# Block maxima, head sums, early weights and step order in a fused attention and two-MoE kernel

## Chip, cores and metric

The kernel runs on one core of a Trainium2 chip, as one program. The metric is device time in microseconds (us), the median of several runs. The profile is one further execution, recorded by the hardware profiler. Engines are called PE (matmuls), DVE (vector), ACT (scalar activation), POOL (GpSimd) and SP (which issues the DMAs).

## What is computed

Three stages follow each other. Block-causal attention over 8 batches, 8 heads, 576 positions and head size 64, whose mask lets a position see its own 64-key block and those before it; its output, read as 4608 tokens of 512 numbers, goes through a soft mixture of experts with 32 slots; and that goes through a two-layer network whose activation is a scaled square of a relu.

```
scores = scale * q @ k.T;  scores = where(block_i >= block_j, scores, -1e9)
attn = softmax(scores);  x = attn @ v                     # 8 batches, 8 heads, 576 x 64
logits = x @ phi                                          # 4608 x 32
d = softmax(logits, over tokens);  slot_input = d.T @ x   # 32 x 512
for e in range(8):                                        # four slots each
    slot_out[e] = relu(slot_input[e] @ w1[e]) @ w2[e]
c = softmax(logits, over slots);  x = c @ slot_out
h = x @ w_in;  out = (s * relu(h) ** 2 + b) @ w_out
```

## The kernel before

**Attention in pairs.** The work of attention is cut into 32 pairs of heads, four pairs to each batch. For a pair, `rough` computes scores of 128-query chunks against the keys in reduced precision, in four pieces r0 to r3, `rough_max` (L289 to L303) takes their maxima on DVE, `rough_join` (L305) joins these into `mx`, and `m_row` turns them into rows `mT` that two small DMAs bring to `mr`. `score` (s0 to s3, L343) then computes the scores that count, `expo` (L350) the exponentials `pc` on ACT, `pv` (L397) the products with the values. POOL adds the exponentials up over keys in `S` (L365 and three pieces at L371 for each pair). The sums are split into two halves of lower precision, `sh` by ACT and `sl` by DVE (L258), and `dens` (L428) reduces them over partitions with matmuls. `tokens` (L415) turns outputs to rows of tokens and multiplies by phi, so that each head brings 64 output numbers and 32 partial logits. `norm` (L439 to L447) divides: `rs`, `rr`, then `xb` (128 rows, four token groups) and `xt` (the last 64 tokens of a batch).

**Maxima.** The maxima of whole 128-key blocks are taken over 128 rows into `mm`. Those 64-key blocks that only the upper 64 queries of a chunk may see are reduced over 64 rows, into the other half of the same tile. Piece r3 lies in the same tile as s1 (`PIG = 1`), and both its maximum on DVE and the exponential of s1 on ACT read that tile.

**Route.** When a batch is done, `route_s0` sums the partial logits of eight heads into `lgs` (L464, one reduce over `xb`, and in odd batches one over `xt`). `route_p` turns it and takes the maxima `mb` and `mt` and the running maximum `nrun`; `route_l` takes exponentials `ex`; `route_e` turns these into `d`; `route_x` multiplies `d` with `xb` and `xt` (L539, L542) and adds into `acc` (L544), with the running sum `ssum`. Odd batches have 128 tokens of two batches in `xt`, and so more of each.

**The order.** The steps of all pairs are written out by hand: `at(tau, ...)` puts each at a time tau, which is 8 for each pair plus an entry of the table `SLOT`, and `run` issues them in order of tau. Each engine works through its instructions in the order in which they were issued, and SP through its DMAs. The words of `w_in` are converted meanwhile, in 16 of the pairs (`wide_in`, ops `ag` and `wi`, L646 and L647 on ACT and L636 and L638 on DVE).

**Expert phase.** After attention, w1 and w2 of the experts (64 half tiles of 512 KB) are loaded by L113 into places that become free: four whole places `wlate`, allocated when attention's buffers are closed, and others after the last steps of attention. The first products with them are `hp` (L922).

Of the kernel before, what the change touches and what calls it, by code (L numbers as in the profile page):

```python
# [34 lines left out]
}  # L35

ON = {"k": "A", "q": "A", "sl": "D"}
# [6 lines left out]
def fused_kernel(  # L44
# [34 lines left out]
    wpre = wholes(ctx, "wpre", NPRE)  # L79

# [12 lines left out]
    wt = {}  # L93

# [48 lines left out]
    XB = rtp.tile([128, 4, 8, 96], F32, name="xb", bufs=1)  # L143
    XT = rtp.tile([128, 8, 96], F32, name="xt", bufs=1)
# [9 lines left out]
    KT, QT, RV = [None] * 3, [None] * 3, [None] * 3  # L154
    for i in (2, 0, 1):
        KT[i] = earlyp.tile([128, 640], F32, name=f"kt_{i}")
        QT[i] = earlyp.tile([128, 640], F32, name=f"qt_{i}")
        RV[i] = earlyp.tile([128, 5, 128], F32, name=f"rv_{i}")
# [3 lines left out]
    NB_ = {"pc": 5, "mT": 4, "ssp": 1}  # L162
# [12 lines left out]
    MM = [latep.tile([128, 2, 5, 2], F32, name=f"mm_{i}") for i in range(2)]  # L175
# [176 lines left out]
    def key_sum(p, c):  # L352
# [4 lines left out]
        if p == NP - 1 and c == 3:  # L357
            sh, sl = st["s3"] = [ring("s" + x, [128, 2, 576], F16)[:, :, 0:256] for x in "hl"]
# [75 lines left out]
    def norm(p):  # L434
# [5 lines left out]
        if p == NP - 1:  # L440
# [3 lines left out]
        DVE.tensor_tensor(out=XB[:, :, 2 * j:2 * j + 2, :], in0=ps[:, :, 0:384].rearrange("p h (u c) -> p u h c", u=4),  # L444
                          in1=rr[:, 0:4].to_broadcast([128, 4, 2, 96]), op=ALU.mult)

        DVE.tensor_tensor(out=XT[l0:l0 + 64, 2 * j:2 * j + 2, :], in0=ps[64:128, :, 384:480],  # L447
                          in1=rr[64:128, 4].to_broadcast([64, 2, 96]), op=ALU.mult)
# [86 lines left out]
    def route_x(b):  # L535
# [5 lines left out]
        if b % 2:  # L541
            PE.matmul(ps[0:32, :], d[:, 128:160], XT[:, :, 0:64], start=False, stop=True)  # L542
# [34 lines left out]
    for p in range(NP):  # L577
# [30 lines left out]
        A("norm", norm)  # L608
        A("mr", m_row)
    for b in range(NB):  # L610
        z = 8 * (4 * b + 3) + O["route"]
        if b == NB - 1:
            at(8 * (NP - 1) + O["den"] + 0.001, 8, route_s0, b, 0, 6)
            at(z + O["rh"], 8, route_s0, b, 6, 8)
        else:
            at(z + O["rh"], 8, route_s0, b)
# [8 lines left out]
    cvp = att.enter_context(tc.tile_pool(name="cvp", bufs=1))  # L625
# [634 lines left out]
```

## Time and profile before

| what | value |
|---|---|
| median of 3 runs | 843.72 us (843.55 to 844.74) |
| the profiled execution | 841.7 us, of which 839.9 are its span |
| PE busy | 780.2 us, 93% of the span |
| DVE, ACT, POOL busy | 681.7, 585.3, 220.2 us |
| attention, expert phase, rest | 0 to 356, 355.5 to 441.5, 442 to 840 us |

The busy shares are means over three stages with different limits, so they say little of one change. The rows below are read by stage: a window gives each engine's busy time in a stretch, a timeline the start and length of each group of instructions and, in brackets, how long its engine was idle before and on whom it waited.

### The profile page before, as it was taken

Reading aid. Unit: us, or ns where it says so; the run is one execution under the profiler, and the core shown is the slowest. Engines: PE = TensorE matmul, PEld = TensorE weight load, DVE = VectorE, ACT = ScalarE, POOL = GpSimd, SP = SyncE. Lnnn points to the kernel's source line nnn. Section 1 sums busy time; section 2 is a strip of 40 time slices with the busy share of each in tenths; the row PEclk is TensorE's granted clock in tenths of the full one; section 3 lists DMA queues with packets and bytes.
Section 4 is the critical chain, followed back from the end, with each engine's and each line's share of the span. In section 5 each row is a group of like instructions: output and inputs, shape, how many; then the busy total and the mean of one; then the engine's idle time right before and its main releaser. Section 6 shows DMA issues by size and latency. Waiting matters only on the chain.

```text
span 839.9 us, 18427 instructions
## 1 busy us (share of the span) xinstructions
PE 780.2 (93%) x7604; PEld 580.5 (69%) x7604; DVE 681.7 (81%) x1175; ACT 585.3 (70%) x848; POOL 220.2 (26%) x191
## 2 busy tenths in 40 slices
PE   4999989898989899967888889999999999999996
PEld 3666757575667575732314678888888888888885
DVE  5788888888888888669876788888888888888885
ACT  4766767575767666547876787777777877877771
POOL 3553534443535344402000011111111111111110
PEclk9999999999999999988899999999999999999999
DMA  4565543242434433299990000000000000000001
GB/s 144 196 211 181 196 145 96 81 159 101 157 133 146 146 96 96 82 385 407 397 392 9 1 26 27 26 27 26 27 26 27 26 27 26 27 26 27 26 27 51
DMA packets 40483, 92.97 MB, mean 111 GB/s; under 512 B 4624, under 2 KB 4944, under 8 KB 40400
## 3 DMA queue, kind: packets, MB, share of 16 engines
q1 hardware_dynamic: 40400, 91.80, 31.3%
q8 instruction: 60, 0.98, 0.5%
q14 instruction: 23, 0.19, 0.1%
HBM read 81.86 MB, written 9.44 MB: 109 GB/s over the span
## 4 chain that ended last, share of the span: by engine, by line
PE 77%; DVE 10%; DMA 8%; ACT 3%; issue 1%; POOL 1%; SPq 0%; POOLq 0%; DVEq 0%; ACTq 0%
PE s L343 13%; PE o L1121 13%; PE o L1123 12%; PE o L1122 12%; PE pv L397 9%; PE tp L415 4%; DMA w<-in_moe_w_dram 4%; PE s L286 4%; PE h L1084 4%; DMA w2h<-in_moe_w_dram 3%; DVE mm L272 3%; DVE lgs L464 2%; PE tp L428 2%; ACT rhl L1102 1%; PE hp L922 1%
## 5 line engine op out<-in xcount | busy, mean ns | idle before, releaser
L272 DVE TENSOR_REDUCE mm<-s 64x4 f32<-64x256 f32 (+5 forms) x224 | 139.1, 634 | 50.2 <-ACT pc L350 30.1
L1103 DVE TENSOR_TENSOR rhl<-G,rhl 128x1792 f16<-128x1792 f32 (+1 forms) x76 | 146.2, 1923 | 3.1 <-ACT rhl L1102 2.7
L350 ACT ACTIVATE pc<-s 128x896 f32<-128x896 f32 (+1 forms) x128 | 104.0, 838 | 58.7 <-PE s L343 30.4
L1085 ACT ACTIVATE r<-h 128x512 f32<-128x512 f32 x144 | 85.8, 596 | 60.8 <-PE h L1084 60.8
L343 PE MATMUL s<-qt,kt 64*128 64x448 f32 (+4 forms) x768 | 124.5, 416 | 1.2 <-DVE mm L272 0.5
L1102 ACT CAST rhl<-G 128x1792 f16<-128x1792 f32 (+1 forms) x76 | 121.0, 1592 | 5.4 <-DVE G L1095 5.3
L365 POOL TENSOR_TENSOR S<-pc 128x896 f32<-128x896 f32 x31 | 64.9, 2093 | 181.8 <-ACT pc L350 181.8
L1123 PEld LDWEIGHTS <-rhl 128*128 128x128 f16 x1008 | 98.8, 98 | 13.2 <-DVE rhl L1103 1.6
L1121 PEld LDWEIGHTS <-rhl 128*128 128x128 f16 x1008 | 98.8, 98 | 13.2
L1122 PEld LDWEIGHTS <-rhl 128*128 128x128 f16 x1008 | 98.8, 98 | 11.8
L397 PE MATMUL pv<-pc,rv 128*64 128x448 f32 (+4 forms) x768 | 100.3, 397 | 0.0
L371 POOL TENSOR_TENSOR S<-S,pc 128x640 f32<-128x640 f32 (+2 forms) x93 | 93.3, 1003 | 7.3
L343 PE MATMUL s<-mr,neg 64*128 64x448 f32 (+4 forms) x384 | 94.9, 487 | 0.0
L1140 POOL TENSOR_TENSOR z<-u,bdif 128x256 f32<-128x256 f32 x18 | 41.8, 2320 | 188.8 <-DVE u L1126 188.8
L1093 DVE TENSOR_TENSOR G<-G 128x512 f32<-128x512 f32 (+1 forms) x76 | 50.5, 665 | 46.5 <-ACT G L1092 46.0
L1092 ACT ACTIVATE G<-r 128x1024 f32<-128x1024 f32 (+1 forms) x76 | 76.9, 1011 | 2.2
L397 PEld LDWEIGHTS pv<-pc,rv 128*64 128x64 f32 x768 | 47.3, 136 | 32.1 <-issue 20.7
L343 PEld LDWEIGHTS s<-qt,kt 64*128 64x128 f32 x768 | 60.4, 188 | 7.4 <-DVE mm L272 2.9
L286 PE MATMUL s<-kr,qr 64*128 64x64 f32 (+4 forms) x384 | 54.0, 348 | 10.2 <-ACT kr L243 7.9
L286 PEld LDWEIGHTS s<-kr,qr 64*128 64x128 f32 x384 | 32.7, 191 | 40.2 <-ACT pc L350 21.1
L1084 PE MATMUL h<-ct,mst 128*128 128x256 f16 x288 | 55.2, 274 | 3.5 <-DVE mst L1049 1.3
L415 PEld LDWEIGHTS tp<-IP,ot 64*128 64x128 f32 x640 | 40.8, 188 | 17.3 <-ACT kr L243 7.3
(302 smaller groups left out, 1787.9 us busy)
## 6 DMA issues: line engine op xcount, KB each, us to landing
w<-in_moe_w_dram SPq DMA_DIRECT2D x36, 512.0 KB
w2h<-in_moe_w_dram SPq DMA_DIRECT2D x28, 512.0 KB
qt<-in_q_dram SPq DMA_DIRECT2D x32, 320.0 KB
kt<-in_k_dram SPq DMA_DIRECT2D x32, 320.0 KB
rv<-in_v_dram SPq DMA_DIRECT2D x32, 320.0 KB
wi<-in_moe_w_in_dram SPq DMA_DIRECT2D x8, 1024.0 KB
wo<-in_moe_w_out_dram SPq DMA_DIRECT2D x8, 1024.0 KB
out_dram<-ob SPq DMA_DIRECT2D x16, 256.0 KB
```

What stands on the lines that cost most here:

```text
L272: DVE.tensor_reduce(out=o, in_=i, axis=AX, op=ALU.max)
L286: PE.matmul(ps[:, h, o:o + k1 - k0], qt[a, 128 * j:128 * j + 128], kt[a, k0:k1], start=(n == 0), stop=(n == len(RG[r]) - 1))
L343: PE.matmul(ps[:, h, o:o + c1 - c0], a[r], b[r], start=(n == 0), stop=(n == 1))
L350: ACT.activation(out=pc[:, :, 0:w], in_=st.pop(("ps", p, c))[:, :, 0:w], func=AF.Exp, scale=scale)
L371: eng.tensor_tensor(out=x, in0=x, in1=pc[:, :, o:o + c1 - c0], op=ALU.add)
L397: PE.matmul(st["pv", p][r, x[0], x[1]], rv[:, sl, r], pc[:, h, o:o + c1 - c0], start=head, stop=(sl == 4 or c1 <= 128))
L1084: PE.matmul(hps[:, 256 * o:256 * o + 256], mst[:, 128 * f:128 * f + 128], ct[g], start=True, stop=True)
L1102: ACT.copy(rh, G)
L1103: DVE.tensor_tensor(out=rl, in0=G, in1=rh, op=ALU.subtract)
L1121: PE.matmul(o, rh[:, a, n], bh, start=first, stop=False)
L1122: PE.matmul(o, rh[:, a, n], bl, start=False, stop=False)
L1123: PE.matmul(o, rl[:, a, n], bh, start=False, stop=last)
```

## The change

Five things are changed.

1. The maxima of 64-key blocks are taken over 128 rows like the others, into a second half `me` of `mm`. `rough_join` becomes one op, the larger of `mm` and `me + mlow`, where `mlow` is -3e38 on the lower 64 rows; it has two inputs in SBUF.
2. `xt` becomes the fifth part of `xb`. A new step `head_sum` adds each pair's partial logits to `la` (pairs 1 to 3 of a batch, 24 adds on DVE, two inputs in SBUF), and `route_s0` is one add of the two halves of `la`. The pieces that the last batch had for this go.
3. Two of the four `wlate` places are allocated from the start, and two whole tiles of w1 (four half tiles) are loaded into them at pairs 26 and 27. Room is made with two buffers in place of three for `rv`, one in place of two for `ag` and for `ot`, and two in place of four for `mT`.
4. All entries of `SLOT` are new.
5. `slotT` is cleared by POOL instead of DVE, and the last pair's `sh` and `sl` of s3 stand in a buffer of `S`.

The diff, cut to its core; of the table a few entries stand:

```diff
 SLOT = {
...
-    5.18176, "sh1": 8.65626, "sl0": 6.52132, "sl1": 8.89128, "pv0": 3.67699, "pv1": 5.43325, "pv2": 5.43402, "pv3":
-    5.78017, "oc": 6.88883, "den": 10.19669, "norm": 11.64578, "route": 12.44301, "re": 2.40618, "rp": 0.37853,
...
+    9.33946, "sl0": 9.95287, "sl1": 10.51401, "pv0": 5.35704, "pv1": 7.37396, "pv2": 8.06025, "pv3": 8.15647, "oc":
+    9.07061, "den": 11.34750, "norm": 14.22647, "hs": 14.23143, "route": 10.06565, "re": 6.23354, "rp": 5.65308,
...
 }
+NEARLY = 2
-ON = {"k": "A", "q": "A", "sl": "D"}
+ON = {"k": "A", "q": "A", "sl": "D", "hs": "D", "xt": "D"}
...
+    wearly = wholes(ctx, "wearly", NEARLY)
...
-    XB = rtp.tile([128, 4, 8, 96], F32, name="xb", bufs=1)
-    XT = rtp.tile([128, 8, 96], F32, name="xt", bufs=1)
+    XB = rtp.tile([128, 5, 8, 96], F32, name="xb", bufs=1)
+    LA = rtp.tile([128, 5, 2, 32], F32, name="la", bufs=1)
...
-        mm, me = MM[p % 2][:, :, :, 0], MM[p % 2][64:128, :, :, 1]
-        by64 = ps[64:128].rearrange("p h (u c) -> p h u c", c=64)
+        mm, me = MM[p % 2][:, 0], MM[p % 2][:, 1]
+        by64 = ps.rearrange("p h (u c) -> p h u c", c=64)
...
-            rmax(me[:, :, 0:1], ps[64:128, :, 448:512])
+            rmax(me[:, :, 0:1], ps[:, :, 448:512])
...
-        rmax(MX[p % 2][:, 0:10], MM[p % 2].rearrange("p h j a -> p (h j) a"))
+        mm, me = (MM[p % 2][:, n].rearrange("p h j -> p (h j)") for n in range(2))
+        DVE.scalar_tensor_tensor(out=MX[p % 2][:, 0:10], in0=me, scalar=mlow[:, 0:1], in1=mm, op0=ALU.add, op1=ALU.max)
...
-        head_sum(lgs[:, gt(b):gt(b) + 4, :], XB[:, :, :, 64:96].rearrange("p u h n -> p u n h"))
-        if b % 2:
-            head_sum(lgs[:, gt(b) + 4, :], XT[:, :, 64:96].rearrange("p h n -> p n h"))
+    def head_sum(p):
+        b, j = p // 4, p % 4
+        if j == 0:
+            return
+        n = 4 + b % 2
+        x = XB[:, 0:n, 2 * j:2 * j + 2, 64:96]
+        eng = {"P": POOL, "D": DVE}["D" if p == NP - 1 else ON["hs"]]
+        eng.tensor_tensor(out=LA[:, 0:n], in0=XB[:, 0:n, 0:2, 64:96] if j == 1 else LA[:, 0:n], in1=x, op=ALU.add)
+    def route_s0(b):
+        n = 4 + b % 2
+        DVE.tensor_tensor(out=lgs[:, gt(b):gt(b) + n, :], in0=LA[:, 0:n, 0], in1=LA[:, 0:n, 1], op=ALU.add)
...
+    early = [split(t) for t in wearly]
+    for i, t in enumerate(early):
+        home["w1", i] = t
+        at(8 * (26 + i), 10, load_w, ("w1", i), t)
...
-    wlate = wholes(ctx, "wlate", 4, reuse_waits="tile")
+    wlate = wearly + wholes(ctx, "wlate", 4 - NEARLY, reuse_waits="tile")
...
-    at(8 * (NP - 1) + O["norm"] + 0.02, 9, DVE.memset, slotT, 0.0)
+    at(8 * (NP - 1) + O["norm"] + 0.02, 9, POOL.memset, slotT, 0.0)
```

**PE, where the fourth batch ends.** In a row on PE before: s is the score tile, kr and qr the rough operands, qt and kt the exact ones; tp takes transposes and route products; a number at the end of a name tells buffers apart.

```order
L286 MATMUL s<-kr_130,qr_132 128x512 x2
L313 MATMUL tp<-idF,lgs 128x64 x2
L494 MATMUL tp<-idF,lgs 32x64 x2
L397 MATMUL pv<-pc,rv_142 64x448 x2
L397 MATMUL pv<-pc,rv_142 64x320 x2
L397 MATMUL pv<-pc,rv_142 64x128 x2
L397 MATMUL pv<-pc,rv_142 64x192 x2
L397 MATMUL pv<-pc,rv_142 64x64 x2
L286 MATMUL s<-kr_130,qr_132 128x192 x2
L286 MATMUL s<-kr_130,qr_132 128x320 x2
L313 MATMUL tp<-idF,ex 128x64 x2
L521 MATMUL tp<-idF,ex 128x64
```

After these stand s0 (L343), its row maxima, and then the products with d (L539, L542).

The same place on PE now:

```order
L311 MATMUL s<-kr_136,qr_138 128x512 x2
L424 MATMUL pv<-pc,rv_145 64x448 x2
L339 MATMUL tp<-idF,lgs 128x64 x2
L516 MATMUL tp<-idF,lgs 32x64 x2
L424 MATMUL pv<-pc,rv_145 64x320 x2
L424 MATMUL pv<-pc,rv_145 64x128 x2
L424 MATMUL pv<-pc,rv_145 64x192 x2
L424 MATMUL pv<-pc,rv_145 64x64 x2
L339 MATMUL tp<-idF,ex 128x64 x2
L543 MATMUL tp<-idF,ex 128x64
L311 MATMUL s<-kr_136,qr_138 128x192 x2
L311 MATMUL s<-kr_136,qr_138 128x320 x2
```

The route transposes have moved behind a group of pv and the transposes of ex ahead of the third rough piece; the products with d follow here, and s0 after them.

**DVE at the same boundary, before**, from the end of `norm` to d:

```order
L272 TENSOR_REDUCE mx_160<-mm_162 128x10
L464 TENSOR_REDUCE lgs<-xb 128x128
L464 TENSOR_REDUCE lgs<-xt 128x32
L272 TENSOR_REDUCE mm_161<-s 128x2
L272 TENSOR_REDUCE mm_161<-s 64x2x2
L497 TENSOR_REDUCE mb<-tp 128x1
L498 SCALAR_TENSOR_TENSOR nrun_112<-mb,nrun_111 128x1
L502 TENSOR_REDUCE mt<-tp 32x1
L503 SCALAR_TENSOR_TENSOR nrun_112<-mt,nrun_112 32x1
L272 TENSOR_REDUCE mm_161<-s 128x2
L258 TENSOR_TENSOR sl<-pc,sh 128x2x128
L525 COPY d<-tp 128x128
```

And now:

```order
L501 TENSOR_TENSOR la<-la,xb 128x320
L297 TENSOR_REDUCE mm_167<-s 128x2
L297 TENSOR_REDUCE mm_167<-s 128x2x2
L506 TENSOR_TENSOR lgs<-la 128x160
L519 TENSOR_REDUCE mb<-tp 128x1
L520 SCALAR_TENSOR_TENSOR nrun_118<-mb,nrun_117 128x1
L524 TENSOR_REDUCE mt<-tp 32x1
L525 SCALAR_TENSOR_TENSOR nrun_118<-mt,nrun_118 32x1
L297 TENSOR_REDUCE mm_167<-s 128x2
L547 COPY d<-tp 128x128
```

The sum has moved behind the reduces of the first piece, and sl out of the way of d.

**DVE in a pair that converts words, before**, in the third pair of that batch:

```order
L258 TENSOR_TENSOR sl<-S,sh 128x2x448
L638 SCALAR_TENSOR_TENSOR wi_634<-wi_772,ag 128x512
L272 TENSOR_REDUCE mm_161<-s 64x2
L439 TENSOR_SCALAR rs_163<-tp 128x10
L443 RECIPROCAL rr<-rs_163 128x10
L444 TENSOR_TENSOR xb<-tp,rr 128x4x192
L447 TENSOR_TENSOR xt<-tp,rr 64x192
L272 TENSOR_REDUCE mx_159<-mm_161 128x10
```

And now:

```order
L283 TENSOR_TENSOR sl<-S,sh 128x2x448
L297 TENSOR_REDUCE mm_167<-s 128x2
L654 SCALAR_TENSOR_TENSOR ag<-ag,wi_874 128x512
L332 SCALAR_TENSOR_TENSOR mx_165<-mm_167,mlow 128x10
L656 SCALAR_TENSOR_TENSOR wi_874<-wi_874,ag 128x512
L466 TENSOR_SCALAR rs_170<-tp 128x10
L470 RECIPROCAL rr<-rs_170 128x10
L471 TENSOR_TENSOR xb<-tp,rr 128x4x192
L479 TENSOR_TENSOR xb<-tp,rr 64x192
L501 TENSOR_TENSOR la<-la,xb 128x320
```

The conversion stands behind the last maximum and ahead of `norm`, with both its ops in one pair, and la closes the pair. On ACT the exponential of s1 now waits for that last maximum; before, the maximum waited for the exponential. On SP the load of a pair's values (rv) stands behind its `mr`, a pair later than before, and of the expert weights four half tiles instead of eight stand between the last pair's loads and those that wait for its last steps.

## Rows read from the trace of the kernel before

**Rows 1.** The page, the chain that ended last: shares of the span.
```profile
PE 77%; DVE 10%; DMA 8%; ACT 3%; issue 1%; POOL 1%; SPq 0%; POOLq 0%; DVEq 0%; ACTq 0%
```

**Rows 2.** Windows: length, busy us of each engine (instructions), granted clock, DMA share, GB/s.
```profile
39.17:49.08 9.91, 9.91 (x116) 7.01 (x116) 8.71 (x16) 7.62 (x14) 5.11 (x4) 1.00 0.62 212
...
49.07:72.84 23.77, 21.62 (x243) 14.45 (x242) 20.00 (x38) 14.64 (x27) 10.19 (x8) 1.00 0.53 180
...
181.60:207.09 25.49, 22.97 (x247) 14.84 (x247) 21.85 (x44) 15.90 (x30) 10.22 (x8) 1.00 0.37 125
...
355.50:441.50 86.00, 68.14 (x549) 26.02 (x548) 68.26 (x135) 61.71 (x92) 4.95 (x7) 0.90 1.02 391
```

**Rows 3.** Waits, 20 to 360 us: engine, line, releaser: total, times, longest.
```profile
PE tp L313 <- DVE lgs L464: 7.7, 7, 1.1
...
PE tp L415 <- DVE acc L544: 6.7, 7, 1.0
```

**Rows 4.** Timeline of PE and DVE, odd boundary: start, us, engine, line, op, count [idle].
```profile
196.28 0.28 PE L313 MATMUL tp<-idF,lgs 64*128 64x64 f32 x2 [1.12 <-DVE lgs L464]
...
199.70 0.28 PE L313 MATMUL tp<-idF,ex 64*128 64x64 f32 x2 [0.23 <-ACT ex L511]
...
200.14 1.02 PE L343 MATMUL s<-qt,kt 64*128 64x448 f32 x4
...
202.18 1.02 PE L542 MATMUL tp<-xt,d 128*32 128x512 f32 x2
...
194.18 1.95 DVE L464 TENSOR_REDUCE lgs<-xb 128x128 f32<-128x1024 f32 x1
...
196.04 0.59 DVE L464 TENSOR_REDUCE lgs<-xt 128x32 f32<-128x256 f32 x1
...
196.66 1.40 DVE L272 TENSOR_REDUCE mm<-s 128x2 f32<-128x768 f32 x2
...
198.09 0.29 DVE L497 TENSOR_REDUCE mb<-tp 128x1 f32<-128x128 f32 x1
...
198.88 1.21 DVE L272 TENSOR_REDUCE mm<-s 128x2 f32<-128x1024 f32 x1
...
200.50 0.28 DVE L525 COPY d<-tp 128x128 f32<-128x128 f32 x1
```

**Rows 5.** Timeline of PE, DVE and POOL, a plain pair.
```profile
41.91 0.50 PE L286 MATMUL s<-kr,qr 64*128 64x448 f32 x4
...
45.19 0.99 PE L343 MATMUL s<-qt,kt 64*128 64x448 f32 x4
...
41.32 0.36 DVE L447 TENSOR_TENSOR xt<-tp,rr 64x192 f32<-64x192 f32 x1
...
42.45 2.66 DVE L272 TENSOR_REDUCE mm<-s 128x2 f32<-128x768 f32 x3 [0.58 <-PE s L286]
...
49.52 2.09 POOL L365 TENSOR_TENSOR S<-pc 128x896 f32<-128x896 f32 x1 [4.56 <-ACT pc L350]
```

**Rows 6.** Groups by form, DVE and POOL, 20 to 356 us: count | busy, mean ns | idle.
```profile
L272 DVE TENSOR_REDUCE mm<-s 64x4 f32<-64x256 f32 x60 | 25.6, 428 | 0.8
...
L272 DVE TENSOR_REDUCE mm<-s 64x2 f32<-64x128 f32 x31 | 9.2, 296 | 30.1 <-ACT pc L350 30.1
...
L258 DVE TENSOR_TENSOR sl<-pc,sh 128x256 f16<-128x256 f32 x31 | 13.2, 426 | 1.3 <-ACT sh L376 1.0
...
L371 POOL TENSOR_TENSOR S<-S,pc 128x640 f32<-128x640 f32 x31 | 48.1, 1551 | 2.4
```

**Rows 7.** Timeline of DVE and POOL, near the end of attention.
```profile
353.21 0.71 DVE L258 TENSOR_TENSOR sl<-pc,sh 128x256 f16<-128x256 f32 x1 [1.03 <-ACT sh L376]
...
353.72 1.60 POOL L371 TENSOR_TENSOR S<-S,pc 128x384 f32<-128x384 f32 x2
```

**Rows 8.** SP's waits, 354 to 366 us, and the window 364 to 366.
```profile
SPq L113 <- PE pv L397: 6.1, 2, 5.8
...
364.00:366.00 2.00, 2.00 (x51) 1.77 (x50) 2.00 (x3) 0.09 (x1) 0.00 (x0) 1.00 0.78 248
```

More of the change, by code (lines that the diff above doesn't have):

```diff
@@ L93, in fused_kernel, with __init__, __getitem__, tile @@
     wt = {}
+    class split:
+        def __init__(self, pool):
+            self.pool, self.t = pool, None
+        def __getitem__(self, h):
+            if h == 0:
+                self.t = self.pool.tile([128, 2048], F32, tag="w", name="w2h")
+            t = self.t
+            class place:
+                def tile(_, shape, dt, tag, name):
+                    return t[:, 1024 * h:1024 * h + 1024]
+            return place()
     def words(key, q0, q1):
@@ L173, in fused_kernel @@
     MX = [latep.tile([128, 128], F32R, name=f"mx_{i}") for i in range(2)]
-    MM = [latep.tile([128, 2, 5, 2], F32, name=f"mm_{i}") for i in range(2)]
+    MM = [latep.tile([128, 2, 2, 5], F32, name=f"mm_{i}") for i in range(2)]
+    mlow = const.tile([128, 1], F32, name="mlow")
     RS = [latep.tile([128, 10], F32, name=f"rs_{i}") for i in range(2)]
@@ L187, in build_rest @@
             POOL.memset(d, -3.0e38)
+        POOL.memset(mlow, 0.0)
+        POOL.memset(mlow[0:64], -3.0e38)
         POOL.memset(EX[32:64, 128:256], 0.0)
@@ L357, in key_sum @@
         if p == NP - 1 and c == 3:
-            sh, sl = st["s3"] = [ring("s" + x, [128, 2, 576], F16)[:, :, 0:256] for x in "hl"]
+            t = ring("S", [128, 2, 448], F32).rearrange("p h c -> p (h c)").bitcast(F16)
+            sh, sl = st["s3"] = [t[:, 512 * x:512 * x + 512].rearrange("p (h c) -> p h c", h=2) for x in range(2)]
             ACT.copy(sh, pc[:, :, 0:256])
@@ L443, in norm @@
         DVE.reciprocal(out=rr.rearrange("p u h a -> p (u h a)"), in_=r)
-        DVE.tensor_tensor(out=XB[:, :, 2 * j:2 * j + 2, :], in0=ps[:, :, 0:384].rearrange("p h (u c) -> p u h c", u=4),
+        DVE.tensor_tensor(out=XB[:, 0:4, 2 * j:2 * j + 2, :], in0=ps[:, :, 0:384].rearrange("p h (u c) -> p u h c", u=4),
                           in1=rr[:, 0:4].to_broadcast([128, 4, 2, 96]), op=ALU.mult)
-        DVE.tensor_tensor(out=XT[l0:l0 + 64, 2 * j:2 * j + 2, :], in0=ps[64:128, :, 384:480],
-                          in1=rr[64:128, 4].to_broadcast([64, 2, 96]), op=ALU.mult)
+        xt = XB[l0:l0 + 64, 4, 2 * j:2 * j + 2, :]
+        if ON["xt"] == "A":
+            for h in range(2):
+                ACT.activation(out=xt[:, h], in_=ps[64:128, h, 384:480], func=AF.Copy, scale=rr[64:128, 4, h, :])
+        else:
+            DVE.tensor_tensor(out=xt, in0=ps[64:128, :, 384:480], in1=rr[64:128, 4].to_broadcast([64, 2, 96]), op=ALU.mult)
         for c in range(4):
@@ L541, in route_x @@
         if b % 2:
-            PE.matmul(ps[0:32, :], d[:, 128:160], XT[:, :, 0:64], start=False, stop=True)
+            PE.matmul(ps[0:32, :], d[:, 128:160], XB[:, 4, :, 0:64], start=False, stop=True)
         f = st["rl", b]
@@ L608, in fused_kernel @@
         A("norm", norm)
+        A("hs", head_sum)
         A("mr", m_row)
@@ L611, in fused_kernel @@
         z = 8 * (4 * b + 3) + O["route"]
[L612 to L616, printed above, removed]
+        at(z + O["rh"], 8, route_s0, b)
         at(z + O["rp"], 8, route_p, b)
@@ L733, in fused_kernel @@
     ready, summed, todo, active = set(), set(), [], []
-    toload = list(wseq[16:])
-    class split:
-        def __init__(self, pool):
-            self.pool, self.t = pool, None
-        def __getitem__(self, h):
-            if h == 0:
-                self.t = self.pool.tile([128, 2048], F32, tag="w", name="w2h")
-            t = self.t
-            class place:
-                def tile(_, shape, dt, tag, name):
-                    return t[:, 1024 * h:1024 * h + 1024]
-            return place()
+    toload = list(wseq[16 + NEARLY:])
     def advance():
@@ L865, in paced @@
         return int(min(n, 8) * CFIRST + max(n - 8, 0) * CLATE)
-    empty = wpost[::-1] + [split(t) for t in wlate[::-1]]
+    empty = wpost[::-1] + [split(t) for t in wlate[:NEARLY - 1:-1]]
     with tc.manual_schedule():
```

34 lines of the change are left out of this document (10 added, 24 removed), and 10 rows, old and new, of the table SLOT.

## Prediction

> **What bounds the kernel now.** I read the page's chain of waits first: 77% of the span ends on PE [rows 1]. Then the windows. The last stage, from 442 us on, the change does not touch, and I carry it over. The question is attention (0 to 356 us) and the expert phase (355.5 to 441.5).
>
> In attention a plain head pair takes 9.91 us and PE is busy for all of it [rows 2]: no saving on DVE, ACT or POOL can shorten such a pair, but a new wait can lengthen it. The pair in which one batch ends and the next goes on is different. Two windows, each a boundary pair and one plain pair, last 23.77 us (even batch) and 25.49 us (odd batch) [rows 2]; less two periods of 9.91 that is 3.95 and 5.67 us extra. With four even and three odd boundaries it makes 32.8 us. The waits show what is late: PE's route transposes wait seven times for lgs, 7.7 us in all, and its token transposes seven times for acc, 6.7 us [rows 3]. Not all of the extra is waiting: the odd boundary has matmuls of its own, the route products that end at 203.20 (1.9 us) and four short transposes [rows 4], some 2.7 us; the even one, with fewer, about 1.4. No order can win more than 32.8 - 4 x 1.4 - 3 x 2.7 = 19 us.
>
> The expert phase is a stream of weights: 86 us at 391 GB/s, DMA share 1.02 [rows 2]. There only bytes taken out of it, or holes in the stream, count.
>
> **Head sums.** Today's lgs stands on DVE ahead of the reduce of the new pair's first score block: 1.95 us and, in odd batches, 0.59 us, from 194.18 to 196.63 [rows 4]. mb follows at 198.09, the running maximum and ex after it, so that ex is transposed at 199.70; d comes at 200.50, behind a reduce of 1.21 us; and PE puts s0 (200.14) ahead of the route products [rows 4]. The change leaves one add of 128x160 here (128x128 in even batches) and puts it behind the first block's reduces; PE does one group of pv before the route transposes, and the route products before s0.
>
> The odd boundary again, from the rows. Its pair starts one period into its window [rows 2], at 191.51. PE begins the first block 2.74 us into a pair (41.91 in the one from 39.17) and DVE takes it up 0.54 later, at 42.45 [rows 5]: here at 194.79. Its two reduces take 1.40 (those from 196.66 [rows 4]), so they end at 196.2, some 196.1 with the maxima at whole height (below). The add I price at 0.30, from the 0.28 of the 128x128 copy d and the 0.43 of a 128x256 op with two inputs [rows 4, 6]; it ends at 196.4. Transposes need 0.6, so mb starts at 197.0. From mb to ex's transposes it is 1.61 now [rows 4]: 198.6. d waits for DVE's 1.21 us reduce, which then ends at 199.1, and takes 0.4; the route products run from 199.5 for 1.9 us, and s0 starts at 201.4. In a plain pair s0 starts 6.02 us into the pair (45.19 in the pair from 39.17 [rows 5]), here at 197.5: 3.9 us extra in place of 5.67. By the same steps the even boundary, without the second pieces, has 2.3 in place of 3.95. Sum: 4 x 1.65 + 3 x 1.75 = **-11.85 us**. acc's work then lies beside s0, so the wait of the tokens goes rather than being next.
>
> In return each batch gets three adds la of 128x256 or 128x320 (24 in all, 0.43 to 0.5 each by the 128x256 row [rows 6]), between xt and the first reduce of the next pair. A hole of 0.58 us stands there now [rows 5], and the work ahead of it can start sooner, because the last maxima stop waiting for exp, for which DVE loses 30.1 us in 31 waits [rows 6]. So la is hidden as long as nothing holds it.
>
> **POOL beside DVE.** This is what speaks against the change. Every DVE op with two inputs in SBUF (sl, ag, wi) stands today where POOL is idle, but one: sl at 353.21 takes 0.71, where the mean is 0.43 [rows 6, 7]. A POOL add was under way that ended just before the next began, at 353.72 [rows 7]. sl ended at 353.92, so its 0.43 began about 353.5: it stood still until POOL's instruction was nearly over, and got in between two of them. The reduces, with one SBUF input or none, run beside POOL in each pair. The Trainium skill, "SBUF — State Buffer", section "Who interferes with whom", says that a DVE instruction with two SBUF inputs and a GpSimd instruction that reads SBUF exclude each other for a whole instruction, and that the one issued first goes first. The one row here that bears on it agrees (0.29 us lost); by the rule alone each op below would wait out whatever add is under way, which is the upper bound that I give from rows.
>
> After the change la, lgs and (in the 16 pairs that convert words) wi meet POOL's adds: 2.09 us, then 1.55, then two in 1.60 together [rows 5, 6, 7]. In a plain pair the exp that feeds POOL now waits for a maximum of 0.30 [rows 6], instead of the reverse, so POOL's first add, at 49.52 today [rows 5], goes to 49.87 and ends at 51.96. la is ready at 50.9 at the earliest (xt ends at 41.68, 51.6 a period later [rows 5], and 0.7 sooner without the wait for exp), waits till 51.85, ends at 52.3; the reduce behind it is due at 52.36. Nothing is lost. Where ag and wi stand ahead of it, I estimate la 0.25 later; the reduces have that much to give, since they end at 45.11 for an s0 at 45.19 today [rows 5] and whole-height maxima free 0.2. I take 0.05 for each of 16 pairs, +0.8, with 0 and 0.2 as bounds (0 to +3.2). At a boundary lgs is ready at 196.0 to 196.1, just where POOL's 1.55 us add ends (by a plain pair's times, 51.96 + 0.08 + 1.55 = 53.6, which is 4.5 into the pair, 196.0): it slips in at no cost, or stands behind the next add, the longer of the two in 1.60, and loses some 0.95. The rows do not tell these apart, and I take half: 7 x 0.45 = **+3.15** (0 to +6.65).
>
> **Maxima at whole height.** Each pair has four reduces over 64 rows, of 0.43 and 0.30 us [rows 6]; I price them the same at 128 rows, since each row has as many elements as before and the 128x256 add takes 0.43 as well [rows 6]. What can be won is the start: of two ops of equal height the second begins 0.08 us before the first ends (196.04 before 194.18 + 1.95 [rows 4]), around the 64-row ops there is no overlap in the trace. Some 0.1 us a side, on DVE, where PE is the bound: 0 on the time (between 0 and the 0.2 used above as slack).
>
> **Two early places.** Four of the 64 half tiles (512 KB each, 2.1 MB) are loaded at pairs 26 and 27, where the DMA engines are busy for 0.6 of a pair [rows 2]. At 391 GB/s that is 5.4 us less stream. But the places are the same four: at the end of attention only two are free, and the next halves wait for pv and sl of the last pair. SP already waits 6.1 us for pv there, and the rate falls to 248 GB/s from 364 to 366 [rows 8]. With only four halves to issue at once (5.4 us of stream from about 356) the engines are empty from 361.5 until a place comes free at 364.2 and bytes flow again at 365: 3.5 to 4 of the 5.4 are lost. Net **-1.6** (0 to -5.4). The last pair's norm and head sums come some 1.4 us sooner, which frees no place that the stream waits for and counts for nothing.
>
> **The rest.** rv goes behind mr in SP's queue with two buffers for three: behind a 1 MB load, 1.4 MB at 391 GB/s are 3.5 us of a pair's 9.91. One ag and one ot buffer: their readers run within the same pair. The memset of slotT goes to POOL, idle there. POOL's 0.35 is paid from the 4.56 us that it is idle per pair [rows 5]. Cost 0; where a cover fails, tenths of a us on up to 31 pairs, which the range holds. Start: within 0.3.
>
> **Sum.** -11.85 + 3.15 + 0.8 - 1.6 = -9.5 us. The profiled run took 841.7 (span 839.9); the median of the runs is 843.72, 2.0 more, and the same gain comes off it: 834.2.
>
> **Rivals.** A: POOL costs nothing and the early weights count in full: -11.85 - 5.4 = -17.2, 826.5; with half of the weights 829. For it: sl did get in between two POOL instructions. Against: the hole follows from the places. Chance 0.12. B: lgs stands behind POOL at all boundaries, the 16 pairs pay 0.2 each and the weights win nothing: -11.85 + 6.65 + 3.2 = -2.0, 841.7; half of it is within 0.2%. Chance 0.13. C, slower: la loses at the border. If POOL's 1.55 us add, queued 0.08 behind the first, goes before la, la ends at 54.0 instead of 52.3; the reduce is 1.7 late, 0.25 is slack, and 24 pairs pay 1.45: +35 on the forecast, 869. It decides from 0.4 us a pair beyond the slack (9.5 / 24). Against it stands the one sl that got in. Chance 0.10. D: the boundary is bound by something behind the route (ssum, tokens), and the change does not do what it says: 843. Chance 0.03.
>
> **Numbers.** The forecast has 0.62. 0.2% is 1.7 us, about what a measurement of this kernel can tell from no change. Faster: 0.62 + 0.12 + half of B, 0.81; same 0.09; slower 0.10. The range leaves out C and half of A: 828.5 to 842.5.
>
> **What would show it.** Plain pairs of 9.91 with PE busy throughout mean that la is hidden; 10.1 or more, with la at 1 us or more, is B or C. The two windows of 23.77 and 25.49 should become about 22.5 and 24.1; lgs at 0.3 or at 1.2 tells which side of the border it fell. A low rate from 361 to 365 confirms the hole; without it, A. If PE waits for exp in plain pairs, the step that made exp later was wrong, and with PE waits behind the route, D.

## The result, and the profile after

The changed kernel takes 835.11 us (833.56 to 835.89), the kernel before in the same comparison 843.95: a ratio of 0.9893, 95% interval 0.988 to 0.9906, some 9 us faster. The forecast was 834.2, in a range from 828.5 to 842.5. The profiled execution took 834.96, 833.2 of them its span. The sum came out; its terms did not, and their errors cancel.

The page of after, first busy time and then the chain that ended last (the second line answers to [rows 1]):

```profile
PE 786.0 (94%) x7604; PEld 581.4 (70%) x7604; DVE 677.2 (81%) x1190; ACT 582.1 (70%) x848; POOL 226.0 (27%) x194
...
PE 78%; DMA 9%; DVE 8%; ACT 2%; issue 1%; POOL 1%; SPq 1%; POOLq 0%; DVEq 0%; ACTq 0%
```

DVE lost two points of the chain, and DMA and SP gained one each. Where that sits, the windows of after tell: length, busy us of each engine (instructions), granted clock, DMA share, GB/s. A plain pair, a boundary pair (even batch) and the plain pair before it, the same for the odd boundary where the fourth batch ends, the expert phase; they answer to [rows 2].

```profile
39.50:49.35 9.85, 9.85 (x117) 6.96 (x115) 8.81 (x18) 6.37 (x12) 5.32 (x4) 1.00 0.61 208
49.35:71.58 22.23, 21.57 (x243) 14.28 (x240) 19.54 (x40) 14.53 (x27) 10.51 (x8) 1.00 0.58 196
176.58:201.36 24.78, 22.63 (x249) 14.59 (x246) 21.38 (x47) 14.73 (x28) 10.80 (x8) 1.00 0.41 133
345.00:434.00 89.00, 73.79 (x547) 27.38 (x546) 65.33 (x131) 61.86 (x92) 6.07 (x9) 0.85 0.96 358
```

Below, a period runs from the fourth score piece (s3) of one pair to that of the next. Boundaries were 13.86 (even) and 15.56 (odd) and are now 12.39, 13.92, 12.21, 14.94, 12.31, 13.76 and 12.21: 102.1 us together have become 91.7. The fourth, in the third window, stands out by 1.1. Plain pairs went from 9.91 to 9.84. The last s3 started at 358.52 and starts at 347.84, 10.7 us sooner (11.2 counted from the second pair, since the start lost 0.5). But from there to the last products of the experts it took 84.9 us and now takes 88.4: the stream of weights gave 3.5 back. The rest after it is 396.5 and 397.0.

The waits of PE from 20 to 360 us (total, times, longest) answer to [rows 3]: the wait for acc is gone, that for lgs is halved.

```profile
PE tp L339 <- DVE lgs L506: 3.8, 7, 1.1
```

DVE and POOL in a plain pair of after: start, length, engine, line, operation, count.

```profile
168.28 0.36 DVE L479 TENSOR_TENSOR xb<-tp,rr 64x192 f32<-64x192 f32 x1
168.68 1.37 DVE L501 TENSOR_TENSOR la<-xb 128x320 f32<-128x320 f32 x1
170.11 2.42 DVE L297 TENSOR_REDUCE mm<-s 128x2 f32<-128x768 f32 x3
...
167.60 2.10 POOL L392 TENSOR_TENSOR S<-pc 128x896 f32<-128x896 f32 x1 [4.32 <-ACT pc L376]
169.78 3.31 POOL L398 TENSOR_TENSOR S<-S,pc 128x640 f32<-128x640 f32 x3
```

And POOL's three adds in the plain pair of [rows 5], before:

```profile
51.69 3.16 POOL L371 TENSOR_TENSOR S<-S,pc 128x640 f32<-128x640 f32 x3
```

la does stand still: it takes 1.37 us, where it takes 0.49 at the end of attention with no POOL add under way. It ends at 170.05, 0.35 after POOL's add of 896 columns (169.70), so it went in ahead of the next add, which is recorded from 169.78 on; the three adds take 3.31 in place of 3.16. The reduces follow at once and the pair takes 9.84, so the wait is hidden. In a pair that converts words it is la's neighbour that meets POOL, and here POOL is the one who waits:

```profile
81.90 0.68 DVE L656 SCALAR_TENSOR_TENSOR wi<-wi,ag 128x512 int32<-128x512 int32 x1
...
84.32 0.57 DVE L501 TENSOR_TENSOR la<-xb 128x320 f32<-128x320 f32 x1
...
82.28 2.27 POOL L392 TENSOR_TENSOR S<-pc 128x896 f32<-128x896 f32 x1 [4.51 <-ACT pc L376]
```

wi was under way when POOL's add was due; the add takes 2.27 in place of 2.10, and la comes so late that it stands for 0.1 only.

### The profile page after: what moved, and what is told of

Same layout as the page of the kernel before. It is cut to its first block, busy times and chain, and to the rows that moved or that the text cites. A ratio compares the mean times of both kernels' runs of the same rounds, so it can differ in the third digit from the quotient of the medians.

```text
span 833.2 us, 18398 instructions
## 1 busy us (share of the span) xinstructions
PE 786.0 (94%) x7604; PEld 581.4 (70%) x7604; DVE 677.2 (81%) x1190; ACT 582.1 (70%) x848; POOL 226.0 (27%) x194
## 4 chain that ended last, share of the span: by engine, by line
PE 78%; DMA 9%; DVE 8%; ACT 2%; issue 1%; POOL 1%; SPq 1%; POOLq 0%; DVEq 0%; ACTq 0%
PE s L369 14%; PE o L1125 13%; PE o L1127 13%; PE o L1126 13%; PE pv L424 8%; PE tp L442 4%; DMA w<-in_moe_w_dram 4%; DMA w2h<-in_moe_w_dram 4%; PE s L311 4%; PE h L1088 4%; DVE mm L297 2%; PE tp L455 2%; ACT rhl L1106 1%; PE tp L561 1%; DMA rv<-in_v_dram 1%
## 5 line engine op out<-in xcount | busy, mean ns | idle before, releaser
L297 DVE TENSOR_REDUCE mm<-s 128x4 f32<-128x256 f32 (+5 forms) x224 | 130.5, 630 | 42.0 <-PE s L311 38.3
L392 POOL TENSOR_TENSOR S<-pc 128x896 f32<-128x896 f32 x31 | 67.6, 2182 | 166.9 <-ACT pc L376 166.9
L398 POOL TENSOR_TENSOR S<-S,pc 128x640 f32<-128x640 f32 (+2 forms) x93 | 95.3, 1025 | 7.3
L369 PEld LDWEIGHTS s<-qt,kt 64*128 64x128 f32 x768 | 61.6, 188 | 10.4 <-issue 5.4
L311 PEld LDWEIGHTS s<-kr,qr 64*128 64x128 f32 x384 | 33.7, 194 | 39.6 <-ACT pc L376 20.4
L369 PEld LDWEIGHTS s<-mr,neg 64*128 64x128 f32 x384 | 39.2, 189 | 15.4 <-issue 10.2
```

The costliest lines, as they stand in the source:

```text
L297: DVE.tensor_reduce(out=o, in_=i, axis=AX, op=ALU.max)
L311: PE.matmul(ps[:, h, o:o + k1 - k0], qt[a, 128 * j:128 * j + 128], kt[a, k0:k1], start=(n == 0), stop=(n == len(RG[r]) - 1))
L369: PE.matmul(ps[:, h, o:o + c1 - c0], a[r], b[r], start=(n == 0), stop=(n == 1))
L398: eng.tensor_tensor(out=x, in0=x, in1=pc[:, :, o:o + c1 - c0], op=ALU.add)
```

## The experiments

Each run is compared with the kernel before on the same chip (medians of before 843.84 to 844.42). The diffs are cut to their core. "Stretch" is the time from the last s3 to the end of the experts' last products.

### Both kernels once more

> The kernel before once more, for a second profile of its expert phase. In the first, that phase took 84.9 us from the last pair's s3 to the end of the experts' last products. All theories: 843.5 to 844.7; if the stream of weights varies by itself from run to run, this stretch differs from 84.9 by 1 us or more.

> The changed kernel once more. In its first profile the stretch from the last pair's s3 to the end of the experts' last products took 88.4 us, 3.5 more than before, where the forecast had 1.6 less. Theory 1 (the hole behind the early places costs more than the two places save): 88 again. Rival (a slow stream or a low clock in that one execution): 84 to 86. Time 833.5 to 836 in both.

Before: 844.37, ratio 0.9998 (0.9988 to 1.0009). Changed: 834.75, 0.9894 (0.9878 to 0.991). In these profiles the last s3 comes at 360.47 and 348.54, and the stretch is 85.5 and 87.6. So attention gained 11 to 12 us and the stretch lost 2.1 to 3.5, in both pairs of profiles: the loss is not one execution's.

### Head sums alone, behind the maxima

To the kernel before only the head sums are added (with `xt` as a part of `xb`); `la` stands behind the join of maxima, and the short add lgs in lgs's old place.

```diff
+    ... "norm": 11.64578, "hs": 12.43840, "route": 12.44301, ...
...
-        head_sum(lgs[:, gt(b):gt(b) + 4, :], XB[:, :, :, 64:96].rearrange("p u h n -> p u n h"))
+        DVE.tensor_tensor(out=lgs[:, gt(b):gt(b) + n, :], in0=LA[:, 0:n, 0], in1=LA[:, 0:n, 1], op=ALU.add)
```

> The kernel before, in its old order, with the head sums alone changed: la behind the join of the maxima, lgs one add behind la, ahead of the first block's reduces. Theory of the port (a DVE op with two SBUF inputs stands still until POOL's add is over): la comes just after POOL's 1.55 us add has begun, ends some 1.1 us late, and 24 pairs pay about 1.1 each: about 865 to 870, la at 1.5 us and more in its row. Rival (no such wait, or only a few tenths): la fits the hole of 0.58 us, boundaries win 1.65 and 2.2: about 831.

848.12, ratio 1.0045 (1.003 to 1.006): slower than before by 4, far from either number, but it shows the race that rival C spoke of. la becomes ready within 0.03 us of the border between POOL's first add and its second. DVE and POOL in two pairs of this run, in the first of which la came first:

```profile
311.12 0.42 DVE L470 TENSOR_TENSOR la<-xb 128x256 f32<-128x256 f32 x1
...
308.93 2.10 POOL L365 TENSOR_TENSOR S<-pc 128x896 f32<-128x896 f32 x1 [4.62 <-ACT pc L350]
311.11 3.44 POOL L371 TENSOR_TENSOR S<-S,pc 128x640 f32<-128x640 f32 x3
...
321.04 1.81 DVE L470 TENSOR_TENSOR la<-la,xb 128x256 f32<-128x256 f32 x1
...
321.01 3.24 POOL L371 TENSOR_TENSOR S<-S,pc 128x640 f32<-128x640 f32 x3
```

At 311.11 both start together, la takes 0.42 and POOL's three adds take 3.44, where they take 3.16 in the kernel before. At 321.01 POOL is 0.03 ahead, and la stands for its whole add: 1.81. Of 22 pairs la won 17 and lost 5. The windows of those two pairs:

```profile
308.41:318.32 9.91, 9.91 (x117) 7.00 (x115) 8.57 (x16) 6.58 (x12) 5.39 (x4) 1.00 0.33 101
318.32:329.41 11.09, 10.17 (x118) 7.02 (x115) 9.89 (x16) 7.74 (x14) 5.17 (x4) 1.00 0.29 91
```

The lost one costs 1.18 us; three boundaries with a lost la took 17.05, 15.99 and 15.99, where the others of their kind take 15.15 and 13.88. And at the boundaries the short lgs stood behind POOL as well, by form (count, busy us, mean ns, idle):

```profile
L475 DVE TENSOR_TENSOR lgs<-la 128x128 f32<-128x128 f32 x4 | 5.5, 1376 | 0.1
```

1.38 us for an add that takes 0.3 when POOL lets it: so even the undisturbed boundaries stayed at 13.88 and 15.15. In this place the sums are worth less than nothing. Whether they would win in another place of the old order was not run.

### No sums spread

The changed kernel without `la`; one reduce over eight heads stands where the new order has lgs.

```diff
+        DVE.tensor_reduce(out=lgs[:, gt(b):gt(b) + n, :], in_=XB[:, 0:n, :, 64:96].rearrange("p u h n -> p u n h"), axis=AX, op=ALU.add)
```

> The changed kernel with the old sum: no la, and lgs as one reduce of 128x1024 (1280 in odd batches) in its new place behind the reduces of the first block. Theory (the sum on the path is what the boundaries lose): lgs ends 1.65 (even) and 2.2 (odd) later, less the 1 us that one boundary lost to POOL: +12, about 846 to 847, boundaries near 14 and 16. Rival (the new order alone makes the gain, the sum is hidden behind it): 835 to 838.

857.48, ratio 1.014 (1.0116 to 1.0165), 10 us more than was expected. By form:

```profile
L506 DVE TENSOR_REDUCE lgs<-xb 128x128 f32<-128x1024 f32 x4 | 7.6, 1897 | 0.1
...
L506 DVE TENSOR_REDUCE lgs<-xb 128x160 f32<-128x1280 f32 x3 | 7.0, 2319 | 0.1
```

The boundaries are 15.42, 15.83, 15.19, 17.87, 15.21, 16.92 and 15.15, 19.9 us more than in the changed kernel: 2.8 each, more than the reduce is longer than the add (1.6 to 2.0); what the rest of it is stays open. The stretch is 91.8, since the last batch's reduce is on the path too. So the two parts are worth little or less than nothing apart (the sums +4, the new order without them +13) and much together.

### Maxima of 64-key blocks back on 64 rows

```diff
-        POOL.memset(mlow[0:64], -3.0e38)
...
-        mm, me = MM[p % 2][:, 0], MM[p % 2][:, 1]
-        by64 = ps.rearrange("p h (u c) -> p h u c", c=64)
+        mm, me = MM[p % 2][:, 0], MM[p % 2][64:128, 1]
+        by64 = ps[64:128].rearrange("p h (u c) -> p h u c", c=64)
```

> The changed kernel with the 64-key maxima back at 64 rows. Forecast's step (only slack, no time): 835 as before, plain pairs 9.84. If the 0.2 us per pair of DVE that it takes back are on the path: plain pairs 9.9 to 10.0, up to +5, and where the later reduce ends behind POOL's border la or lgs show it.

842.3, ratio 0.9982 (0.9971 to 0.9993): 7 us of the 9 are gone. A plain pair and one that converts words, in windows:

```profile
170.68:180.59 9.91, 9.91 (x117) 7.01 (x114) 9.08 (x16) 7.59 (x14) 5.24 (x4) 1.00 0.57 190
180.59:190.79 10.20, 10.14 (x117) 7.01 (x114) 9.42 (x18) 7.71 (x14) 5.58 (x4) 1.00 0.59 203
```

The plain pair takes 9.91 as before the change, the converting one 10.20, and the boundaries add up to 96.9 in place of 91.7. So most of the gain hangs on this part, which was priced at 0, as it hangs on the sums above: la fills the hole ahead of the reduces, and the whole-height maxima make room for it.

### Whole-height maxima alone

The kernel before with `mm`, `me`, `mlow` and `rough_join` of the change and nothing else.

```diff
+    mlow = const.tile([128, 1], F32, name="mlow")
...
-            rmax(me[:, :, 0:1], ps[64:128, :, 448:512])
+            rmax(me[:, :, 0:1], ps[:, :, 448:512])
```

> The kernel before with the maxima at whole height alone: old order, old sums, old memory. In the changed kernel the same step was worth 7.4 (842.3 against 834.9). Forecast's step (only slack): 843.5 to 844. Theory (the slack is used by what the new order puts into DVE, the old order has less use for it): -1 to -2, plain pairs 9.84 for 9.91, boundaries 0.1 shorter. Rival (the maxima win by themselves): -5 to -7, 837 to 839.

842.94 beside 844.42, ratio 0.9983 (0.9973 to 0.9993): 1.4 us, which is the small gain expected, but it is made of a larger one and a loss. A plain pair:

```profile
171.01:180.85 9.84, 9.84 (x118) 6.95 (x115) 7.86 (x15) 6.60 (x12) 5.09 (x4) 1.00 0.56 182
```

9.84 in place of 9.91, boundaries 0.3 less: from the second pair to the last s3 attention gained 3.4 to 4.4 us (by the two profiles of before).

Why a pair in which PE is busy throughout could become shorter at all, the start of s0 tells: DVE's reduces, the load of s0's first weights (PEld) and its first matmuls on PE, before and in this run.

```profile
175.93 1.69 DVE L272 TENSOR_REDUCE mm<-s 64x4 f32<-64x256 f32 x2
177.67 0.19 PEld L343 LDWEIGHTS s<-qt,kt 64*128 64x128 f32 x2
177.70 0.62 PE L343 MATMUL s<-qt,kt 64*128 64x448 f32 x2
```

```profile
174.37 2.42 DVE L275 TENSOR_REDUCE mm<-s 128x2 f32<-128x768 f32 x3 [0.65 <-PE s L289]
176.97 0.19 PEld L347 LDWEIGHTS s<-qt,kt 64*128 64x128 f32 x2
177.12 0.54 PE L347 MATMUL s<-qt,kt 64*128 64x448 f32 x2
```

Before, the load comes 0.05 us behind the last reduce (177.62), and s0's first matmuls, recorded from 0.16 before their weights are there, take 0.62. With the maxima at whole height the reduces end at 176.79, the load follows 0.18 later, and the matmuls take 0.54: that 0.08 is the difference between the two pairs. So PE did wait for DVE, and its row shows that wait as busy.

The stretch lost 2.1 to 2.7 of it: 87.6, although order and buffers are those of before. That the rate of the stream fell here too, to 393 GB/s, pointed to what this kernel shares with the changed one, `mlow`.

### Early places: none, one

The second run has 1 in place of the 0.

```diff
-NEARLY = 2
+NEARLY = 0
```

> The changed kernel without the early places: no place is allocated all through attention, all 64 half tiles are loaded after it. The forecast's term (early places worth 1.6, at most 5.4): 836.7, at most 840.5. Rival (the hole costs more than the places save): 832 to 834, and the stretch from the last s3 to the end of the experts back at some 85 us.

> The changed kernel with one early place instead of two: two half tiles early (1 MB, 2.7 us of stream), six instead of four that can be issued at once at the end of attention. Theory of the hole: the stream is empty for some 2.7 us less, so the time stays within 0.5 of the changed kernel, 834.5 to 835.5. Rival (early bytes count in full, no hole that matters): +2.7, 837.5.

None: 835.81, 0.9899 (0.9886 to 0.9913). One: 834.29, 0.9877 (0.9859 to 0.9895). By ratios and by medians two places are worth 0.4 to 1.1 us against none, which the intervals do not tell from nothing, and nothing against one. In the stretch they are worth nothing: 88.5 with none and with one, 88.4 and 87.6 with two. So the hole does not cost more than the places save, and without them the stretch does not fall back to 85. The stream of the changed kernel, in windows 4 to 8 and 18 to 22 us after its last s3, shows where 2.1 MB of head start went:

```profile
351.84:353.84 2.00, 1.40 (x20) 1.09 (x18) 2.00 (x5) 1.54 (x3) 0.00 (x0) 1.00 0.03 12
353.84:355.84 2.00, 1.89 (x48) 1.70 (x48) 0.66 (x2) 0.00 (x0) 0.00 (x0) 1.00 0.65 172
...
365.84:367.84 2.00, 1.46 (x7) 1.46 (x8) 0.49 (x1) 1.07 (x2) 0.00 (x0) 0.50 0.69 180
367.84:369.84 2.00, 1.56 (x11) 0.72 (x14) 1.43 (x2) 0.00 (x0) 0.00 (x0) 0.50 0.88 281
```

Twice the rate falls, and SP's waits from 340 to 372 us name both doors; the third row is the second door in the kernel before (360 to 378 us):

```profile
SPq L132 <- DVE sl L283: 7.4, 1, 7.4
SPq L132 <- PE s L564: 7.0, 1, 7.0
```

```profile
SPq L113 <- PE s L539: 4.7, 1, 4.7
```

The first is the hole that the forecast named: four halves issued, then nothing until sl of the last pair. The second was not in it: the next places come free with the last batch's route products (L564, L539 before), and a stream that is 2.1 MB ahead waits there 2.3 us longer.

### The old buffers

Three buffers for `rv`, two for `ag` and `ot`, four for `mT`, no early places; the rest of the change stays.

> The changed kernel without anything of its part on memory: no early places, three rv, two ag, two ot and four mT buffers as before; order, head sums and maxima are the new ones. The stream of weights ran at 400 GB/s from 26 to 76 us after the last s3 in the kernel before and at 392 to 394 in all variants of the changed one, the one without early places too. If the smaller buffers or their places are the reason: 400 again, and about 834.5. If the order is: 393, and 835 to 836.

835.07, ratio 0.9895 (0.9876 to 0.9913): as the changed kernel. The third part of the change is worth nothing that these runs can tell, and the stream still ran at 393 GB/s: neither the smaller buffers nor the early places slow it.

### lgs without the shared port

lgs as a reduce, which has one input, over la's two halves, ahead of the 64-key maxima of the new pair's first piece.

```diff
+            if p >= 6 and (p - 6) % 4 == 0:
+                route_s0((p - 6) // 4)
...
-        DVE.tensor_tensor(out=lgs[:, gt(b):gt(b) + n, :], in0=LA[:, 0:n, 0], in1=LA[:, 0:n, 1], op=ALU.add)
+        DVE.tensor_reduce(out=lgs[:, gt(b):gt(b) + n, :], in_=LA[:, 0:n].rearrange("p u s n -> p u n s"), axis=AX, op=ALU.add)
```

> The changed kernel with lgs as a reduce of the two halves of la (one input in SBUF, 128x256 or 128x320) and ahead of the 64-key maxima instead of behind them. Theory of the port: an op with one SBUF input does not wait for POOL, so lgs takes 0.43 to 0.5 at every boundary, the fourth boundary (14.94) falls to 13.8, the others by 0.2: -2, about 833. Rival (lgs was late for another reason): the fourth boundary stays at 14.9, and the time is the same or 1 us more.

833.48, ratio 0.9873 (0.9854 to 0.9891), at most 1 to 2 us better, with intervals that overlap. It acts mainly on the boundary that stood out; the others gained 0 to 0.1. In the changed kernel the wait for POOL there had a cause of its own; PE, DVE and POOL at the fourth boundary, then DVE at the fifth:

```profile
188.86 0.97 PE L424 MATMUL pv<-pc,rv 128*64 128x448 f32 x4 [0.47 <-DMA rv<-in_v_dram]
...
190.30 1.29 DVE L297 TENSOR_REDUCE mm<-s 128x2 f32<-128x768 f32 x2 [0.43 <-PE s L311]
191.51 1.04 DVE L506 TENSOR_TENSOR lgs<-la 128x160 f32<-128x160 f32 x1
...
191.37 0.99 POOL L398 TENSOR_TENSOR S<-S,pc 128x384 f32<-128x384 f32 x1
...
234.31 1.29 DVE L297 TENSOR_REDUCE mm<-s 128x2 f32<-128x768 f32 x2
235.51 0.31 DVE L506 TENSOR_TENSOR lgs<-la 128x128 f32<-128x128 f32 x1
```

The pair's values (rv) landed late, PE waited 0.47, the first block and its reduces came 0.43 late, and lgs, ready 4.6 us into the pair elsewhere, came at 5.09: 0.13 after POOL had begun its next add (4.96). It stood still until that ended. In the run with a free lgs the boundary takes 14.30 in place of 14.94, lgs 0.48 and not 1.04; what is left over the 13.75 to 13.92 of the other odd ones is the late rv, whose wait PE shows there too (0.5 us). In the repeat of the changed kernel rv came 1.06 late at this place, lgs with it (5.69, between two adds, 0.43), and the boundary took 14.93 all the same. The kernel before has no wait of PE for rv.

### Both of the last

> The changed kernel with lgs as a reduce with one input ahead of the 64-key maxima, and one early place instead of two. Each alone took 833.5 and 834.3 where the changed kernel took 834.8 to 835.1. If they add: 832.5 to 833; if the early places are worth nothing either way: 833.5.

lgs without the port and one early place: 833.99, ratio 0.9883 (0.9861 to 0.9904). The two do not add up, as far as runs between 831.51 and 836.22 can tell.

### The weights' places at multiples of 256 bytes

`mlow` holds four bytes in each partition and takes 32, in a pool that lies ahead of all the others. So in the kernel before the four whole places (tile w2h, for 28 of the 64 half tiles) start at byte 108800 (425 x 256) of each partition and on, all at multiples of 256, and in the changed one at 108832 and on. The other places lie 160 or 224 bytes beyond such a multiple before, 192 or 224 now. This run is the free lgs with padding only: `mlow` as wide as 256 bytes, and a pad ahead of each of the two groups of places.

```diff
-    mlow = const.tile([128, 1], F32, name="mlow")
+    mlow = const.tile([128, 64], F32, name="mlow")
...
+    later(ph2, "padl", 1).tile([128, 24], F32, name="padl")
...
+    later(ph2, "padr", 1, "right").tile([128, 56], F32, name="padr")
```

> The variant with lgs as a one-input reduce ahead of the 64-key maxima, with three pads of 252, 96 and 224 bytes per partition, so that every place for expert weights begins at a multiple of 256 bytes. In the kernel before four places do (108800 and on), and their w2 half tiles stream in 1.28 us each against 1.35 for the other places; in the changed kernel mlow lies in front of all of them and moves them by 32 bytes, and all 32 half tiles of w2 take 1.35. Theory (the start address sets the rate): 1.28 for all of them, 400 GB/s or more from 26 to 76 us after the last s3, the time 2 to 2.5 below that variant's 833.5: about 831. Rival (the rate has another cause): 1.35, 393 GB/s, 833.5.

830.04, ratio 0.9833 (0.9819 to 0.9847), the best of all versions and better than both kernels. The steady part of the stream, 26 to 76 us after the last s3, in four runs: before, changed, whole-height maxima alone, aligned.

```profile
384.50:434.50 50.00, 40.71 (x321) 13.13 (x310) 44.28 (x88) 45.09 (x67) 4.65 (x4) 0.93 1.04 401
```

```profile
373.84:423.84 50.00, 43.26 (x317) 13.66 (x310) 43.59 (x88) 44.80 (x66) 4.58 (x4) 0.89 1.04 392
```

```profile
381.72:431.72 50.00, 40.38 (x298) 13.07 (x296) 44.03 (x91) 44.50 (x65) 4.65 (x4) 0.90 1.04 393
```

```profile
373.31:423.31 50.00, 41.78 (x318) 13.26 (x310) 44.16 (x86) 45.30 (x68) 4.57 (x4) 0.90 1.04 410
```

The DMA share is 1.04 in all four, the last number differs: at the same occupancy 401, 392, 393 and 410 GB/s. In these windows a packet of 2 KB takes 84.2 ns in the mean where all places are aligned and 88.3 where none is (86.6 in the kernel before, where some are); a half tile of 512 KB takes 1.28 and 1.35 us. The stretch falls from 87.95 (free lgs) to 84.6, which is all of the 3.4 us between the two medians. All ten profiles with the small `mlow`, in old or new order and with old or new buffers, have 391 to 394; the three without it (before, its repeat, the head sums alone) have 401; and padding alone gives 410. So that the address is the cause is shown. The granted clock is not the cause: it stood at the lower of its two levels (1.2 GHz) for 20.4 us of the stretch in the repeat of before (85.5), with none and with one early place (88.5), with the free lgs (88.0) and here (84.6). Which offsets cost how much is not shown: in the kernel before, most half tiles of w2 at 160 and 224 bytes run at 88 ns, but some three at 160 run at 84 to 86; and whether multiples of 128 would do was not run.

The Trainium skill, "DMA: Bandwidth & Descriptors", section "How a descriptor splits into AXI transactions", says that a descriptor (the order to move one run of bytes) is cut into pieces of 256 bytes that start at multiples of 256, and that a read which starts elsewhere fetches bytes it does not use. By that rule a read of 2 KB that starts 32 bytes off costs 65 units of 32 bytes in place of 64, an estimate of 1.6% from that page. The direction agrees. The size does not: these packets, whose shifted side is the one written, cost 4.1 ns of 84.2, 4.9%.

## Why the prediction was right, and where it was not

| term | forecast | measured |
|---|---|---|
| boundaries, POOL's part included | -11.85 + 3.15 = -8.7 | -10.4 |
| pairs between boundaries | 0 | 24 x -0.07, less some 0.9 where loads were late |
| of them, the 16 that convert words | +0.8 | 0 more |
| last s3 to the experts' end | -1.6 | +2.1 to +3.5 |
| start and rest | within 0.3 | about +1 |
| sum | -9.5 | -6.7 and -8.7 (two pairs of profiles), -9 (medians) |

**Boundaries.** The working from the rows held: 2.3 and 3.9 us extra were forecast with the port free, and six of the seven boundaries have 2.4 to 2.6 and 3.9 to 4.1 over a pair of 9.84. The wait for acc went and nothing took its place, so rival D is out.

**POOL at the boundary.** The rule was right and the half of it a poor choice: lgs was ready just ahead of POOL's border (4.56 to 4.70 us into the pair, the end of POOL's add at 4.62 to 4.88) and slipped in six times of seven, at 0.28 to 0.35 us. The term was 3.15 where 0.6 was paid. The Trainium skill, "SBUF — State Buffer", section "Who interferes with whom", has the one that issues first go first, for a whole instruction. The pairs above agree, in both directions (la 1.81 behind POOL, POOL 2.27 behind wi).

**la.** Hidden, as forecast, at 1.37 us in plain pairs. I had named 1 us or more as a sign of B or C together with pairs of 10.1; the pairs are 9.84, so the wait is there and costs nothing. The 16 converting pairs pay nothing, since wi holds POOL up and not the reverse. What rival C feared happens in the kernel with the sums alone: there the border was lost 5 times in 22, at up to 2.1 us.

**Maxima at whole height.** The failed step of attention. "On DVE, where PE is the bound: 0" rests on the reading that PE is busy for all of a plain pair, so that no saving on DVE can shorten it. But s0's weights wait for the last reduce, 0.08 us that PE's row counts as busy, so DVE was bounding the same pairs; the 45.11 and 45.19 of the working had the two side by side. Alone they give 0.07 a pair and 0.3 a boundary; in the new order, with la in the pair, 7 us.

**rv behind mr.** Priced at 0 with 3.5 us of 9.91 as its cover. At one boundary, where a 1 MB load stood ahead, the cover failed: 0.5 to 1.1 us, and in the profiled run the delay pushed lgs over POOL's border. Three buffers in place of two did not help (four waits, 3.0 us, in the run with the old buffers). That leaves the place in SP's queue; no run moved it back. mr is later too: s0's weights waited for it 0.3 and 1.0 us in all in the two profiles of before, 2.5 and 3.2 in those of the changed kernel.

**The weights.** The sign was wrong. Of the 5.4 us of head start I had 3.5 to 4 lost at the first hole; the second door, the route products, took nearly all that was left. And the rate of the whole stream fell by 2%, from the address of a tile of four bytes, which neither the diff nor an order of instructions shows. I had carried 391 GB/s over as a constant. The 64 half tiles (33.5 MB) at 392 in place of 401 GB/s are 1.9 us, an estimate from the steady windows: more than half of what the stretch lost.

**The sum** came this close by luck: 1.7 too little hoped from the boundaries (2.5 too much for POOL, 0.8 too much gain from the route), 0.8 too much for the converting pairs and a net 0.8 too little from plain pairs stand against 4 to 5 too much hoped from the weights. The 0.5 to 1.1 that the last stage took longer goes with the granted clock: behind the experts, the last 5 us of the run left out, it stood at 1.2 GHz for 3.4 us in both profiles of before and for 6.8 in both of the changed kernel. In all fourteen profiles the rest is 396.1 to 396.8 with 3.4, 397.0 to 398.3 with 6.8 and 399.0 with 10.2; no run changes the clock alone. The 0.5 at the start did not recur in the repeat.

## What to carry to other kernels

Where two engines exclude each other, ask not whether an operation meets the other engine but at which instant it becomes ready, against the border between two of the other's instructions: a few hundredths of a microsecond decided between 0.42 and 1.81, and one late load elsewhere moved an operation across. An engine whose work ends 0.1 us before the bound goes on may be a bound too: a busy row does not show it, the load of the next weights does. What is saved there counts for more once something else is put into the slack. A small new tile ahead of large ones shifts them all: see where the targets of a long stream start, and pad them back.

## What the runs showed of the hardware that was not expected

Two effects. With all destinations off a multiple of 256 bytes (by 32, 192 or 224) a 2 KB packet cost 4.9% more than with all on one, at the same DMA share (1.04), and the stream ran at 392 GB/s against 410, with 401 where 28 of the 64 half tiles were on one. And DVE could get in between two POOL instructions that are 0.08 us apart: in the plain pair above POOL's next add waited for no input that the profile shows, and la, which had stood for most of a microsecond, still went first.
